# Row maxima of an attention kernel, turned by VectorE and stored by SyncE

## The chip, the cores and the metric

The kernel runs on one core of a Trainium2 chip. Five engines work side by side, each through its own list of instructions, in order: TensorE (PE, matrix products, with its weight loads shown as PEld), VectorE (DVE), ScalarE (ACT), GpSimd (POOL) and SyncE (SP, which only issues transfers). Semaphores tie them together. The metric is the device time of one execution in microseconds.

## The reference

Four layers are applied in turn, each to the layer norm of a residual stream `x` of 2048 rows and 512 columns, 32 heads of 16 columns. Layers 1 and 3 are linear attention with a learned softmax feature map; layers 2 and 4 are attention in four segments of 512 rows with a memory carried from segment to segment. The change lies in layers 2 and 4:

```
logits = jnp.einsum("bhqd,bhkd->bhqk", qs, ks) * scale + mask
p = _softmax(logits, axis=-1)
a_dot = jnp.einsum("bhqk,bhkd->bhqd", p, vs)
...
o = g * a_mem + (1.0 - g) * a_dot
```

All numbers are float32. Products that need the precision are made of a high and a low part (`hi`, `lo`; `hh`, `hl`; `oh`, `ol`), as three products.

## The kernel before, in words

**Stages.** Layer 1 (`LayerA`) makes a first pass over the rows for its sums and a second for its outputs, up to some 290 us of the profile; layer 2 (`LayerB.steps`) runs from there to some 690 us; layers 3 and 4 repeat it. The outputs of the last segment of one layer, and the first pass of the next, are done inside its neighbours.

**Slots and periods.** `LayerB.steps` counts slots `k`. Five slots make a period. A period serves one unit `m`: four heads of one segment, 32 units a layer (8 a segment). In its period, `attend` multiplies keys and queries (tile `lg`, five products, one in each slot), ScalarE takes the exponential (`P`), GpSimd clears what lies above the diagonal, and in slot 0 of the next period `weighted` multiplies by the values. Into the gaps go the projections, outputs and norms that the tables `FIRST`, `GAPS`, `LAST` and `FINAL` name: "5.2 V+/6" stands for period 5 of the segment, slot 2. The order in which the program calls an engine is the order in which it runs (`Ordered`, `held`): nothing is reordered later.

**The maxima.** The softmax needs each row's largest logit. `maxima` computes the same logits ten slots ahead of `attend`, in two pairs of PSUM banks in turn: `mx` and `my` in slots 0, 1 and 3, two of the four `g` banks in slots 2 and 4. DVE takes the maximum of each (`CUSTOM_DVE_ANT_0`, with `mxs` as the result, one column of 16 for each head and block of rows). `put_maxima` then has PE turn the 128x16 tile into 16 rows of 128 in a `g` bank; ScalarE copies them with the sign changed into `mt` (one buffer), and one slot later issues the transfer of `mt` into rows 63 and 127 of the tile `Q` of queries (shown as `e`). There the product of `attend` subtracts them, since the rows of `K` in that place hold ones. A put in slot 0 of one period is needed in slot 0 of the next.

**SyncE's list.** Six transfers a period (`stack`, slots 1 and 2, `e<-ta`) lay the parts of queries and keys in place for `attend`. Besides these it loads weights (`wqk`), rows and residuals, and stores rows. Each transfer takes the next of eight semaphores in turn and waits for the transfer that had it before.

**Paired products.** `mm3_pair` runs two products in the upper and lower 64 rows of PE. Where the two change places, at two points of 24 steps, a `sync.nop` waits for PE, and PE's next matmul waits for that `nop` (L464). So PE also waits for whatever stands ahead of it in SyncE's list.

**Residual sums.** `out_pair` multiplies by the output weights; ScalarE copies the result, GpSimd adds it to the residual two slots later, and SyncE stores the sum four slots later. The two rows of a pair are `xr` and `mmq`.

**The weights `awv`.** In layer 3's first pass, which runs inside layer 2's last segment, `load_w("awv")` issues eight loads at once ahead of the last four steps of the norm.

Of the kernel before, what the change touches and what calls it, by code (L numbers as in the profile page):

```python
# [7 lines left out]
F32 = mybir.dt.float32  # L8
F32R = mybir.dt.float32r
BF16 = mybir.dt.bfloat16  # L10
AF = mybir.ActivationFunctionType
# [4 lines left out]
D = 512  # L16
H = 32
DH = 16
P = 128
NSEG = 4  # L20
# [11 lines left out]
MT = 1  # L32
G = 4
# [68 lines left out]
def interleave_kernel(ctx, tc, x_in, a_wqkv, a_wphi, a_wo, b_wq, b_wk, b_wv, b_wo, b_beta,  # L102
                      c_ident, c_mask, c_bd, out):
    nc = tc.nc
    MUL, ADD, SUB, MAX, MIN = ALU.mult, ALU.add, ALU.subtract, ALU.max, ALU.min
# [14 lines left out]
    def T2(tag, bufs, dt=F32, shape=(P, 512)):  # L120
        return sp.tile(list(shape), dt, tag=tag, bufs=bufs, name=nm(tag))

    def PS(tag, bufs, shape=(P, 512)):
        return ps.tile(list(shape), F32, tag=tag, bufs=bufs, name=nm(tag))
# [38 lines left out]
    dve, act, pool, sync = [Ordered(e) for e in (nc.vector, nc.scalar, nc.gpsimd, nc.sync)]  # L163
# [15 lines left out]
    def tp(*a):  # L179
        work[0] += 108  # L180
        return held(nc.tensor.transpose(*a))  # L181
# [4 lines left out]
    ident = cp.tile([P, P], F32, name="ident")  # L186
    bd = cp.tile([P, 27], F32, name="bd")
# [39 lines left out]
    def load_w(key, src=None, tag="w8", low=dve):  # L227
        w = []
        for _ in bring(w, key, src, tag, low):
            pass  # L230
        return w
# [269 lines left out]
        wait(end)  # L501
        yield

    def out_pair(tiles, xdst, w, soon, w0=0, w1=D):

        pos = [PS("g", G) for _ in tiles]

        def side(po, o):
            return po[:, 0 : w1 - w0], o, lambda b, kc: w[b][:, kc, w0:w1]

        yield from mm3_pair(*[side(po, o) for po, (x, i, o) in zip(pos, tiles)])
        for po, (x, i, o) in zip(pos, tiles):
            y = T2("tb3", TB3)[:, 0 : w1 - w0]
            act.copy(y, po[:, 0 : w1 - w0])
            soon(2, lambda x=x, y=y: pool.tensor_tensor(out=x[:, w0:w1], in0=y, in1=x[:, w0:w1], op=ADD))
            if w1 == D:
                soon(4, lambda x=x, i=i: sync.dma_start(out=xdst[i], in_=x))
        yield

    def weigh(out, p, eps, add, eng=pool):  # L520
# [16 lines left out]
    def v_tile(hT, w, vv, tag, order=range(4), pairs=False):  # L537
        v = sp.tile([P, 4, VROW], F32, tag="v", bufs=2, name=nm("v"))
        vv[:] = [v]
        pool.memset(v[:, :, 0 : H * VW].rearrange("p t (h e) -> p t h e", e=VW)[:, :, :, DH : DH + 1], 1.0)  # L540
        pool.memset(v[:, :, H * VW : VROW], 0.0)
        if not pairs:
            for t in order:
                po = PS(*tag)
                yield from tok_proj(po, hT, t, w)
                act.copy(v[:, t, 0 : H * VW].rearrange("p (h e) -> p h e", e=VW)[:, :, 0:DH],
                         po.rearrange("p (h e) -> p h e", e=DH))
                yield
            return
        for ts in (order[0:2], order[2:4]):  # L550
            for n in range(pairs):
                pos = [PS(*tag) for _ in ts]
                w0, w1 = D * n // pairs, D * (n + 1) // pairs

                def side(po, t):
                    po, lhs, rhs = tok_side(po, hT, t, w)
                    return po[:, 0 : w1 - w0], lhs, lambda b, kc: rhs(b, kc)[:, w0:w1]

                yield from mm3_pair(*[side(po, t) for po, t in zip(pos, ts)])
                for po, t in zip(pos, ts):  # L560
                    act.copy(v[:, t, w0 // DH * VW : w1 // DH * VW].rearrange("p (h e) -> p h e", e=VW)[:, :, 0:DH],
                             po[:, 0 : w1 - w0].rearrange("p (h e) -> p h e", e=DH))
                yield
# [80 lines left out]
    class LayerA:  # L644
# [65 lines left out]
        def pass1(self, first):  # L710
# [8 lines left out]
            if first:  # L719
                wq, wk, wv, upc = self.first(hTs, vv, upcoming)  # L720
            else:
                norm = norm_T(self.xsrc, SEGS[0], hTs, slow=True, off=True)
                for _ in range(11):
                    next(norm)
                    yield
                wv = load_w("awv")
                for _ in norm:
                    yield
                vt = v_tile(hTs, wv, vv, ("g", G), pairs=1)

                def values():
                    for _ in range(3):
                        next(vt)

                for _ in range(5):
                    values()
                    yield
                upc = upcoming(1, False)
                next(upc[1])
                for _ in range(3):  # L740
                    values()
                    yield
                for n in range(8):
                    values()
                    yield
                wk = load_w("awk", None, "e8")
                yield
            self.mmq = [T2("mmq", 2, shape=(P, NT // 2, 2, H)) for _ in range(2)]
            kva = sp.tile([P, 8, VW], F32, tag="acc", bufs=1, name=nm("kva"))
            late = None  # L750
            for n, s in enumerate(SEGS):
# [51 lines left out]
                if n < NSEG - 1:  # L803
                    hTs, g = upc
# [176 lines left out]
    class LayerB:  # L981
# [6 lines left out]
        def start(self):  # L988
            mem = sp.tile([P, NC, 10 * VW], F32, tag="acc", bufs=1, name=nm("mem"))
            self.acc, self.kn = mem[:, :, 0 : 2 * VW], mem[:, :, 2 * VW :]  # L990
            self.sets = []
            for b in range(NSET):
                Q, K = [T2("e8", 2 * NSET, F32R, (P, 4, 512)) for _ in range(2)]
                self.sets.append((Q, K))
                for t, rows in ((Q, mask[0:32, 0:P]), (K, ones)):
                    dma(t[3:P:4].rearrange("p a t -> p (a t)"), rows.unsqueeze(1).broadcast_to([32, 16, P]))
                    yield
# [152 lines left out]
        def maxima(self, m):  # L1150


            s, c, hf = m // 8, m % 8 // 2, m % 2
            Q, K = [t[:, 2 * hf : 2 * hf + 2, :] for t in self.st[s, c]["set"]]
            mx = T2("mxs", 2, shape=(P, 16))

            def prod(pb, r, i, at, w):
                for e in range(2):
                    q, k = Q[64 * e : 64 * e + 63, r, :], K[64 * e : 64 * e + 63, r, :]
                    mm(pb[e][:, at : at + w], lhsT=q[:, i * P : (i + 1) * P], rhs=k[:, 0:w],  # L1160
                       start=True, stop=True, tile_position=(64 * e, 0))

            def top(pb, e, r, i, at):
                n = (i + 1) * P
                col = (e * 2 + r) * 4 + i
                pl = pb[e][:, at : at + n]
                with tc.high_priority():
                    dve.tensor_tensor_reduce(
                        out=pl, in0=pl, in1=mask[:, 512 - n : 512], scale=1.0, scalar=-3.0e38,
                        op0=ADD, op1=MAX, accum_out=mx[:, col : col + 1])  # L1170

            for what in ([(0, 0, 0), (0, 2, P)], [(0, 3, 0)], [(1, 0, 0), (1, 2, P)],
                         [(0, 1, 0), (1, 1, 256)], [(1, 3, 0)]):
                if self.k % R in SPARE if self.k >= 0 else self.k % 2:
                    pb = [PS("g", G) for _ in range(2)]
                else:
                    pb = [PS(t, 1) for t in ("mx", "my")]
                for r, i, at in what:
                    prod(pb, r, i, at, max(256, (i + 1) * P))
                for r, i, at in what:  # L1180
                    for e in range(2):
                        top(pb, e, r, i, at)
                self.mx[m] = mx
                yield

        def put_maxima(self, m):
            s, c, hf = m // 8, m % 8 // 2, m % 2
            Q = self.st[s, c]["set"][0][:, 2 * hf : 2 * hf + 2, :]
            pt = PS("g", G)
            tp(pt[0:16, 0:P], self.mx.pop(m), ident)  # L1190
            mt = T2("mt", MT, F32R, shape=(16, P))
            act.activation(mt, pt[0:16, 0:P], AF.Copy, scale=-1.0)
            self.later.append(lambda: act.dma_start(out=Q[63:P:64].bitcast(F32), in_=mt.bitcast(F32)))

        def attend(self, m):

# [119 lines left out]
        def out(self, s):  # L1316
            layer, i = (self.layer, NT - 4) if s < 0 else (self, 4 * s)
            for t in (0, 2):
                tiles = [(x, i + t + n, oT) for n, (oT, x) in enumerate(self.turned[0:2])]
                del self.turned[0:2]  # L1320
                parts = 2 if self.thin and s == NSEG - 2 else 1
                for n in range(parts):
                    yield from out_pair(tiles, layer.xdst, layer.wo, lambda late, f: self.at.setdefault(self.k + late, []).append(f),
                                        n * D // parts, (n + 1) * D // parts)

        def early(self):
# [269 lines left out]
```

## Time and profile before

| | us |
|---|---|
| median of three runs | 1345.33 |
| lowest and highest | 1339.39, 1346.64 |
| profiled execution | 1346.11 |
| its span, first to last instruction | 1344.4 |
| granted TensorE clock | 0.993 |
| PE, DVE, ACT, POOL busy | 1283.6, 1037.1, 845.2, 752.0 |

A group's row gives its line, engine, operation, written and read tiles and count, then busy time and the mean of one, then idle time of the engine just before and what ended it. Since a helper (L155, L177, L181) records the instructions, tiles tell more than lines. In a timeline row the first number is the start, the second the length of the merged instructions, and the bracket the idle time before them. "SPq" and "ACTq" are the issue of transfers. Matmuls overlap; their ends are modelled.

### The profile page before, as it was taken

What the parts mean: (1) busy time and instruction counts of PE and PEld (TensorE: products, weight loads), DVE (VectorE), ACT (ScalarE), POOL (GpSimd) and SP (SyncE); (2) the same over time, 40 slices, a digit from 0 to 9 for tenths busy, and PEclk for the clock granted to TensorE, in tenths of its full rate; (3) what the DMA queues carried; (4) which work ended last, traced back from release to release, by engine and by line L of the source; (5) the groups of instructions that cost most, each with busy time, mean ns of one, the idle gap of its engine ahead of it and who ended that gap; (6) DMA issues with size and microseconds to landing.
All of it is one profiled execution on the core that took longest, in us unless ns stands there. A gap on an engine that the chain in (4) does not pass through costs nothing.

```text
span 1344.4 us, 41913 instructions
## 1 busy us (share of the span) xinstructions
PE 1283.6 (95%) x16552; PEld 995.0 (74%) x16552; DVE 1037.1 (77%) x3247; ACT 845.2 (63%) x1274; POOL 752.0 (56%) x1116
## 2 busy tenths in 40 slices
PE   7999989999999999999899998999999999999987
PEld 6887868867777777776668886786767777777664
DVE  4766778688888888887667676797788788788884
ACT  5556445647787787686544433464768877877754
POOL 1568765315667667665325355561456666766643
PEclk9999999999999999999999998999999999999999
DMA  6398437535555544545350103646446554454422
GB/s 207 103 336 259 174 119 233 177 110 144 166 178 145 152 122 141 155 128 163 94 190 29 64 33 127 216 152 184 132 139 188 154 164 109 141 140 111 120 69 79
DMA packets 134419, 196.58 MB, mean 146 GB/s; under 512 B 15440, under 2 KB 61648, under 8 KB 133456
## 3 DMA queue, kind: packets, MB, share of 16 engines
q1 hardware_dynamic: 132256, 193.27, 47.6%
q8 instruction: 131, 2.15, 0.7%
q10 hardware_dynamic: 1968, 0.64, 0.2%
q14 instruction: 64, 0.52, 0.1%
HBM read 101.05 MB, written 39.85 MB: 105 GB/s over the span
## 4 chain that ended last, share of the span: by engine, by line
PE 74%; DVE 13%; ACT 4%; DMA 3%; issue 3%; POOL 2%; SPq 1%; ACTq 0%; DVEq 0%; POOLq 0%
PE g L177 58%; PE lg L177 6%; PE g L181 4%; PE mx L177 3%; DVE g L155 3%; PE lg L181 2%; DVE U L155 2%; DVE mx L155 1%; DVE my L155 1%; PE my L177 1%; ACT P L155 1%; SPq L155 1%; DVE es L155 1%; DVE mxs L155 1%; POOL P L155 1%
## 5 line engine op out<-in xcount | busy, mean ns | idle before, releaser
L155 ACT ACTIVATE P<-lg 128x1024 f32<-128x1024 f32 x316 | 321.4, 1017 | 91.6 <-PE lg L177 73.0
L155 POOL TENSOR_SCALAR_AFFINE_SELECT P<-P 128x256 f32<-128x256 f32 (+1 forms) x448 | 189.8, 442 | 265.8 <-ACT P L155 240.0
L155 DVE CUSTOM_DVE_ANT_0 mx<-mx,mask 128x512 f32<-128x512 f32 (+2 forms) x316 | 159.1, 503 | 82.6 <-PE my L177 67.5
L155 DVE CUSTOM_DVE_ANT_0 g<-g,mask 128x128 f32<-128x128 f32 (+3 forms) x392 | 189.3, 538 | 7.2 <-PE g L177 6.9
L177 PE MATMUL g<-hh,wqk 64*128 64x512 f32 (+1 forms) x960 | 183.2, 394 | 3.7 <-SPq L155 3.7
L177 PE MATMUL g<-w,oh 64*128 64x512 f32 (+2 forms) x848 | 162.0, 380 | 2.6 <-ACT oh L155 2.6
L155 DVE CUSTOM_DVE_ANT_0 my<-my,mask 128x512 f32<-128x512 f32 (+2 forms) x316 | 164.0, 519 | 0.0
L177 PE MATMUL g<-P,v 128*32 128x128 f32 (+3 forms) x2064 | 153.1, 436 | 3.0 <-DVE hl L155 1.6
L177 PE MATMUL lg<-e,e 64*128 64x512 f32 (+1 forms) x1010 | 145.6, 343 | 9.7 <-ACT P L155 9.7
L177 PE MATMUL g<-w,hh 64*128 64x512 f32 (+1 forms) x672 | 143.4, 395 | 5.3 <-SPq L155 3.3
L155 DVE DVE_READ_ACCUMULATOR2_ANT mxs<- 128x1 f32 x1024 | 144.1, 141 | 0.0
L177 PEld LDWEIGHTS lg<-e,e 64*128 64x128 f32 x1010 | 92.8, 185 | 53.5 <-ACT P L155 21.5
L177 PEld LDWEIGHTS g<-hh,wqk 64*128 64x128 f32 (+1 forms) x960 | 99.4, 185 | 24.2 <-SPq L155 6.4
L177 PEld LDWEIGHTS g<-P,v 128*32 128x32 f32 x2064 | 65.9, 110 | 65.6 <-issue 59.8
L177 PEld LDWEIGHTS g<-w,oh 64*128 64x128 f32 (+1 forms) x848 | 95.1, 187 | 19.4 <-ACT oh L155 3.5
L177 PE MATMUL g<-w,ol 64*128 64x512 f32 (+2 forms) x424 | 101.8, 377 | 0.6 <-DVE ol L155 0.5
L155 ACT COPY tb<-g 128x512 f32<-128x512 f32 (+1 forms) x132 | 71.1, 575 | 49.1 <-PE g L177 48.7
L177 PE MATMUL g<-hl,wqk 64*128 64x512 f32 (+1 forms) x480 | 101.6, 390 | 0.0
L177 PEld LDWEIGHTS g<-w,hh 64*128 64x128 f32 (+1 forms) x672 | 83.8, 188 | 21.2 <-SPq L155 3.6
L177 PE MATMUL g<-w,hl 64*128 64x512 f32 (+1 forms) x336 | 89.6, 393 | 0.9 <-issue 0.9
L155 DVE TENSOR_REDUCE es<-P 128x64 f32<-128x1024 f32 x64 | 77.4, 1209 | 13.3 <-ACT P L155 13.3
L177 PE MATMUL g<-e,e 63*128 63x256 f32 (+3 forms) x488 | 83.0, 350 | 0.9 <-DVE mxs L155 0.9
(164 smaller groups left out, 2930.3 us busy)
## 6 DMA issues: line engine op xcount, KB each, us to landing
e<-ta SPq DMA_DIRECT2D x384, 128.0 KB
wqk<-wqk SPq DMA_DIRECT2D x128, 256.0 KB
x<-x SPq DMA_DIRECT2D x48, 256.0 KB
pq<-tb SPq DMA_DIRECT2D x24, 256.0 KB
tb<-pq SPq DMA_DIRECT2D x24, 256.0 KB
x<-xr SPq DMA_DIRECT2D x22, 256.0 KB
xr<-x SPq DMA_DIRECT2D x20, 256.0 KB
x<-in SPq DMA_DIRECT2D x16, 256.0 KB
```

The lines of the kernel that those rows point to most:

```text
L155: i = f(*a, **k)
L177: return held(nc.tensor.matmul(*a, **k))
L181: return held(nc.tensor.transpose(*a))
```

## The change

**Maxima.** `maxima` now writes into one of two tiles of 128x32 that are cleared once a layer (`tops`). `put_maxima` has DVE turn four blocks of 32x32 into one 32x128 tile `mt`, in place of PE and ScalarE. SyncE issues the transfer of its first 16 rows three slots later, in place of ScalarE one slot later. The sign moves into `K`: its rows hold minus one.

**Residual sums.** `out_pair` gets the delays from outside: 2 and 5 slots (add, store) for the outputs of segments up to the second, in place of 2 and 4; 1 and 2 slots for those of the third, which run in the last segment.

**`awv`.** Its eight loads go out two at a time, behind the last four steps of the norm.

```diff
-    def out_pair(tiles, xdst, w, soon, w0=0, w1=D):
+    def out_pair(tiles, xdst, w, soon, late, w0=0, w1=D):
...
-            soon(2, lambda x=x, y=y: pool.tensor_tensor(out=x[:, w0:w1], in0=y, in1=x[:, w0:w1], op=ADD))
+            soon(late[0], lambda x=x, y=y: pool.tensor_tensor(out=x[:, w0:w1], in0=y, in1=x[:, w0:w1], op=ADD))
             if w1 == D:
-                soon(4, lambda x=x, i=i: sync.dma_start(out=xdst[i], in_=x))
+                soon(late[1], lambda x=x, i=i: sync.dma_start(out=xdst[i], in_=x))
...
-                wv = load_w("awv")
+                wv = []
+                weights = bring(wv, "awv")
                 for _ in norm:
+                    next(weights, None)
                     yield
+                for _ in weights:
+                    pass
...
+            self.tops = [T2("mxs", 2, shape=(P, 32)) for _ in range(2)]
+            for t in self.tops:
+                pool.memset(t, 0.0)
...
-            mx = T2("mxs", 2, shape=(P, 16))
+            mx = self.tops[m % 2]
...
-            pt = PS("g", G)
-            tp(pt[0:16, 0:P], self.mx.pop(m), ident)
-            mt = T2("mt", MT, F32R, shape=(16, P))
-            act.activation(mt, pt[0:16, 0:P], AF.Copy, scale=-1.0)
-            self.later.append(lambda: act.dma_start(out=Q[63:P:64].bitcast(F32), in_=mt.bitcast(F32)))
+            mt, mx = T2("mt", MT, shape=(32, P)), self.mx.pop(m)
+            for b in range(4):
+                dve.transpose(out=mt[:, 32 * b : 32 * b + 32], in_=mx[32 * b : 32 * b + 32, :])
+            self.at.setdefault(self.k + 3, []).append(
+                lambda: sync.dma_start(out=Q[63:P:64].bitcast(F32), in_=mt[0:16]))
...
+                                        (2, 5) if s < NSEG - 2 else (1, 2),
...
-    bd[[15, 31], 25] = 1.0
+    bd[[15, 31], 25] = -1.0
```

How the change moves instructions, at the places that the prediction speaks of. On PE, slot 0 of a period in layer 2 (near 410 us of the profile), before: the first products of the next unit's maxima, two groups of other turns, the turn of the maxima, the readings of the memory, the values.

```order
L177 MATMUL my_5953<-e_432_2744,e_431_2743 128x384
L181 MATMUL g_5964<-ident,x_4740 128x128 x4
L181 MATMUL g_5971<-ident,tb_922_5218 128x128 x4
L181 MATMUL g_5980<-ident,mxs_5687 16x128
L177 MATMUL g_5984<-mem_2742,tb_918_5212 32x34 x32
L177 MATMUL g_6027<-P_999_5684,v_4868 32x512 x2
```

The fourth row is gone from PE. On DVE, the same place as it stands now: the reductions of slot 0, a low part, the new turns, the weighing of the readings, and the reductions of slot 1.

```order
L155 ISA my_5955,mxs_2743<-my_5955,mask 128x384
L155 ISA mxs_2743 128x1
L155 TENSOR_TENSOR hl_5965<-g_5966,hh_5964 128x4x128
L155 STREAM_TRANSPOSE mt_5982<-mxs_2744 32x32 x4
L155 TENSOR_SCALAR r_6020<-g_5987 128x16
L155 RECIPROCAL r_6020<-r_6020 128x16
L155 TENSOR_TENSOR ot_5714<-g_5987,r_6020 128x256
L155 TENSOR_TENSOR mem_2742<-g_6049,mem_2742 128x34
L155 ISA mx_6076,mxs_2743<-mx_6076,mask 128x512
```

The turns read `mxs` of the unit before; the reductions around them write the other tile. All else stands as before. On SyncE, period 4 of layer 2's third segment (near 545 us), before:

```order
L155 DMA e_451_2825<-ta_1379_7937 32x2x512
L155 DMA x_6_104<-mmq_8226 128x512
L155 DMA x_7_105<-xr_8228 128x512
L155 DMA wqk_2393<-wqk_80 128x2x256
L155 DMA wqk_2394<-wqk_81 128x2x256
L155 DMA x_8659<-x_4_102 128x512
```

and now:

```order
L155 DMA e_453_2829<-ta_1342_7940 32x2x512
L155 DMA e_433_2747<-mt_8462 2x8x128
L155 DMA wqk_2393<-wqk_80 128x2x256
L155 DMA wqk_2394<-wqk_81 128x2x256
L155 DMA x_6_104<-mmq_8228 128x512
L155 DMA x_7_105<-xr_8230 128x512
L155 DMA x_8662<-x_4_102 128x512
```

Ahead of the two loads of weights there stands one store of maxima in place of two stores of residual sums, which went behind them.

## The prediction

> **What bounds the kernel now.** I read the page first (engines, chain), then the stages, then the tiles `mxs` and `mt` that the change takes off TensorE and ScalarE, then the waits, then single stretches of the timeline.
>
> ```profile
> span 1344.4 us, 41913 instructions
> PE 1283.6 (95%) x16552; PEld 995.0 (74%) x16552; DVE 1037.1 (77%) x3247; ACT 845.2 (63%) x1274; POOL 752.0 (56%) x1116
> PE 74%; DVE 13%; ACT 4%; DMA 3%; issue 3%; POOL 2%; SPq 1%; ACTq 0%; DVEq 0%; POOLq 0%
> ```
>
> TensorE is busy 95% of the span and carries 74% of the chain of waits. The stages say the same of the two attention layers (one call of windows; the columns are length, PE, PEld, DVE, ACT and POOL busy, granted clock, DMA share, GB/s):
>
> ```profile
> 300.00:650.00 350.00, 339.59 (x5079) 259.37 (x5076) 292.22 (x1117) 267.05 (x397) 225.74 (x368) 1.00 0.53 151
> 960.00:1250.00 290.00, 283.54 (x4249) 217.06 (x4247) 240.77 (x930) 222.99 (x330) 188.54 (x310) 1.00 0.51 143
> 1250.00:1320.00 70.00, 60.23 (x1020) 43.29 (x1018) 55.99 (x212) 43.43 (x65) 36.65 (x60) 0.98 0.35 100
> ```
>
> PE is idle 10.4 of 350 us and 6.5 of 290 us; only the last 70 us leave 9.8 us. So what shortens PE's own list shortens the kernel almost one for one, and a stall counts if PE itself stood still. DVE is the second engine: 83% of the first two stages (292.22/350, 240.77/290), with 57.8 and 49.2 us free. The whole change lies in attention, so its worth is read there.
>
> **Part 1, the transpose leaves PE.** 64 times PE turned a 128x16 tile of maxima:
>
> ```profile
> L181 PE MATMUL g<-ident,mxs x64: 272/273/278, 282.9 to 1314.0; 128*16 128x128 f32 x64
>   DVE mxs L155: 22.8, 29
> 409.68 0.60 PE L181 MATMUL g<-ident,tb 128*128 128x128 f32 x4
> 410.12 0.27 PE L181 MATMUL g<-ident,mxs 128*16 128x128 f32 x1
> 410.32 0.77 PE L177 MATMUL g<-mem,tb 128*32 128x34 f32 x64
> ```
>
> Matmuls overlap, so 273 ns is not the price; the distance of starts is. Four turns from 409.68 to 410.12 are 0.11 us each; from this one to the next matmul it is 0.20, but that step (to narrow weights) would follow the turn before it as well. I take 0.11: 64 x 0.11 = **7.0 us**; with 0.20 it would be 12.8, the upper end.
>
> The second row says what PE's matmuls and weight loads together waited for ahead of this turn: 22.8 us in 29 times for DVE's last maxima. Most of it lay beside a matmul still running. PE itself stood still this long (columns: total us, times, longest):
>
> ```profile
> PE g L181 <- DVE mxs L155: 9.1, 11, 1.6
> PE g L177 <- SPq L155: 7.0, 6, 3.3
> DVE mx L155 <- PE my L177: 67.5, 85, 3.2
> 373.65 0.28 PE L181 MATMUL g<-ident,mxs 128*16 128x128 f32 x1 [0.62 <-DVE mxs L155]
> 1277.58 0.28 PE L181 MATMUL g<-ident,mxs 128*16 128x128 f32 x1 [1.58 <-DVE mxs L155]
> ```
>
> 9.1 us in 11 waits. Without the turn PE runs on to the readings of the memory and the weighted values, some 3 us of work, before slot 1 asks for a bank that DVE must have emptied. DVE is no faster, so a part comes back there: I count **7 us** of the 9.1 as gained (0 if every wait only moves; 12 if the modelled tail of the matmul ahead, up to 0.28 us in each of the 11, was idle too).
>
> **Part 2, DVE does it.** 256 instructions of 32x32 are new. The nearest rows:
>
> ```profile
> L155 DVE STREAM_TRANSPOSE U<-U 128x512 f32<-128x512 f32 x63 | 44.5, 707 | 10.6 <-ACT U L155 10.6
> L155 DVE STREAM_TRANSPOSE U<-U 128x256 f32<-128x256 f32 x2 | 0.9, 446 | 3.8 <-ACT U L155 3.7
> 39.14 0.69 DVE L155 COPY share<-gates 32x8 f32<-32x8 f32 x4
> 525.89 0.70 DVE L155 CUSTOM_DVE_ANT_0 mx<-mx,mask 128x512 f32<-128x512 f32 x1 [1.26 <-PE my L177]
> ```
>
> From 512 to 256 columns a transpose loses 261 ns, 1.02 ns a column; 32 columns would take 446 - 224 x 1.02 = 218 ns, four of them 0.87 us. Four independent copies on 32 partitions took 0.69 us. I take 0.75 us for a put of the maxima, 48 us over 64 (44 to 56). They stand behind slot 0's reductions and ahead of slot 1's, just where DVE waits for PE: the last row shows 1.26 us of it, and the waits row 67.5 us in 85 times. So 48 us go into 107 us of idle time in two stages that also have the third. I charge **+2 us** for periods where DVE was late already (at 373.65 it was statistics of rows that delayed it); 0 is the lower bound, and the upper bound is the rival below. Where the cover is gone, it costs 0.75 us a period.
>
> The four transposes also wait for the one `mt` buffer, which is free once the store before has landed: issued in slot 3, two slots ahead. What is queued behind them on DVE is the reductions of slot 1, and for those PE waits through the banks.
>
> **Part 3, ScalarE and its store.**
>
> ```profile
> L155 ACT ACTIVATE mt<-g x64: 257/261/268, 283.3 to 1314.4; 16x128 fp32r<-16x128 f32 x64
> L155 ACTq DMA_DIRECT2D e<-mt x64: 505/520/1373, 283.6 to 1317.8; - x64
> 605.47 3.67 SPq L155 DMA_DIRECT2D w<-awv  x8
> 610.16 7.69 SPq L155 DMA_DIRECT2D e<-ta  x6
> 614.64 0.52 ACTq L155 DMA_DIRECT2D e<-mt  x1
> 615.20 1.29 ACT L155 ACTIVATE tb<-tb 128x512 f32<-128x512 f32 x2 [2.13 <-DMA w<-awv]
> 617.46 0.57 PE L177 MATMUL lg<-e,e 64*128 64x256 f32 x4 [2.06 <-ACT P L155]
> ```
>
> 64 x 0.26 = 16.7 us leave ACT, which is 76% busy in these stages and not the bound: no gain of its own. But the stretch from 605 shows a stall. Eight loads of `awv` go out in 3.67 us; ScalarE's store of the maxima then waits for a transfer of that burst (2.13 us idle), the exponentials behind it are late, and PE stands 2.06 us. The change takes both away: the store is no longer on ScalarE, and the loads go out as two, two and four in three periods. **2 us** gained (0 to 2.1). What they feed is asked for only some slots later.
>
> **Part 4, SyncE's queue.** It takes the 64 stores, 0.52 us each on ScalarE's queue (its neighbours' issue has a median of 0.59, the row of `e<-ta` below). That would be idle business, were it not for L464: the halves of a paired product are separated by an empty instruction on SyncE, and PE waits for it when the queue is behind. These are the 7.0 us in 6 waits above. Three of them:
>
> ```profile
> 542.00 0.53 SPq L155 DMA_DIRECT2D x<-mmq  x1
> 542.78 1.41 SPq L155 DMA_DIRECT2D x<-xr  x1
> 544.28 0.94 SPq L155 DMA_DIRECT2D wqk<-wqk  x2
> 545.33 0.50 PE L177 MATMUL g<-hh,wqk 64*128 64x512 f32 x2 [0.97 <-SPq L155]
> 1000.02 0.53 SPq L155 DMA_DIRECT2D x<-mmq  x1
> 1000.82 2.10 SPq L155 DMA_DIRECT2D x<-xr  x1
> 1004.06 0.50 PE L177 MATMUL g<-hh,wqk 64*128 64x512 f32 x2 [1.68 <-SPq L155]
> 642.45 0.53 SPq L155 DMA_DIRECT2D x<-mmq  x1
> 643.61 4.37 SPq L155 DMA_DIRECT2D x<-x  x4
> 648.08 0.50 PE L177 MATMUL g<-w,hh 64*128 64x512 f32 x2 [3.28 <-SPq L155]
> L155 SPq DMA_DIRECT2D e<-ta x384: 526/589/1698, 255.3 to 1296.5; - x192
> ```
>
> At 545 and 1004 the stores of two residual sums (0.53 + 1.41 and 0.53 + 2.10 us) stand ahead of the weights' loads and the empty instruction. A slot later they stand behind it, and one store of maxima (0.5) takes their place: 1.0 + 1.6 us gained. At 648 four loads of rows take 4.37 us, and two of them read rows whose stores went out 1 to 2 us earlier (642.45); in the last segment the change issues these stores two slots earlier, ahead of six stack transfers, so I count 2 of the 3.28 us. Against it: the other three waits (1.1 us together) and those empty instructions that had less than 0.55 us to spare get the new 0.5 us; I charge 2 us. Net **2.5 us** gained (from 5 lost to 6 gained).
>
> **Sum:** 7.0 + 7 - 2 + 2 + 2.5 = 16.5 us. The profiled execution took 1346.11 us, 1.7 over its span and 0.8 over the median of the runs shown: 1346.1 - 16.5 = 1329.6, and 1328.8 beside the median. I say **1328**.
>
> **Rivals.** First, the waits only move: DVE has 48 us more to do and PE's 9.1 us come back at the banks of slots 1 and 3, with SyncE's gains eaten by its new stores. What is left is 7.0 + 2 - 2 = 7: 1339. For it: DVE at 83% goes to 90%. Against: the 67.5 us in which DVE waits for PE. The Trainium skill (Perfetto Trace Analysis, Optimizing Scalar/DVE Operations) holds that many small instructions cost a saturated VectorE throughput, which speaks for this one; no row here shows DVE saturated in the long stages.
>
> Second, slower: SyncE's queue becomes the bound. If the store of slot 3 delays the second empty instruction of every period, PE waits 0.55 us in some 60 of the 64 periods: 33 us lost, against 14 gained in parts 1 to 3 and 4.6 at the three places. That is 14.4 slower than 1345.3, about 1360. It decides from the point where SyncE comes less than 0.55 us ahead of PE. Against: only 6 waits now, and 384 x 0.59 + 128 x 0.47 = 287 us of issue in some 745 us of attention leave SyncE waiting most of the time. The Trainium skill (Perfetto Trace Analysis, DMA Optimizations) advises to spread transfers over the issuing engines where an issuer is the bottleneck, the opposite of this step; its condition is not met by these rows.
>
> Third, all of it comes: every one of the 9.1 us, 0.2 us a turn (12.8), 2, 6 and no charge on DVE: 30 us, 1316.
>
> That the change doesn't do it is excluded: no transpose of `mxs` and no store on ScalarE stands in the new order.
>
> **Chances.** Forecast (1320 to 1337) 0.55, third (below 1320) 0.19, first (1337 to 1344) 0.16, second 0.10. The range takes in the third's end and the first: 1314 to 1343. A measurement of this kernel tells about 0.5%, 6.7 us, from no change, so faster means below 1338.6: 0.55 + 0.19 and a quarter of the first's, 0.78; same, the rest of the first's, 0.12; slower 0.10.
>
> **What would show it.** Right: four DVE transposes of about 0.2 us each in every period, no `mxs` among what PE waits for at L181, PE's waits for SyncE below 4 us, the periods near 545, 612 and 1004 shorter by 1 to 2 us, and an ordinary period shorter by 0.1. Wrong: new waits of PE for `mxs` at `mx`, `my` or `g` of 5 us and more (the first rival), waits for SyncE above 10 us (the second), or the first product of a period (`lg<-e,e`) waiting for the transfer of `mt`, which I priced at nothing because it has two slots to land.

## The result, and the profile after

The changed kernel takes 1330.23 us (median of 4 runs, 1329.09 to 1334.12), beside 1345.99 us for the kernel before (1339.39 to 1348.97). The ratio is 0.9895, 95% interval 0.9853 to 0.9937: faster, by about 16 us. The profiled execution, the slowest of the four, took 1334.12 us with a span of 1332.4 us, 12.0 us under the span before. The number came out close to the forecast, but not by the forecast's sum, as the trace shows.

The page of the changed kernel: span, busy time by engine, chain by engine. Then its three stages of the attention layers (length, PE, PEld, DVE, ACT and POOL busy, granted clock, DMA share, GB/s):

```profile
span 1332.4 us, 41983 instructions
...
PE 1276.0 (96%) x16488; PEld 989.9 (74%) x16488; DVE 1077.4 (81%) x3503; ACT 834.8 (63%) x1210; POOL 752.4 (56%) x1120
...
PE 75%; DVE 16%; ACT 3%; issue 3%; DMA 2%; POOL 1%; SPq 1%; DVEq 0%; ACTq 0%; POOLq 0%
```

```profile
300.00:650.00 350.00, 346.49 (x5228) 264.32 (x5226) 318.58 (x1269) 269.16 (x378) 228.51 (x375) 1.00 0.54 154
960.00:1250.00 290.00, 288.61 (x4412) 221.44 (x4406) 263.41 (x1054) 227.03 (x320) 195.89 (x319) 1.00 0.53 149
1250.00:1320.00 70.00, 62.98 (x1004) 45.69 (x1002) 57.51 (x216) 45.53 (x62) 39.24 (x68) 1.00 0.32 87
```

In the first two stages PE is idle 3.5 of 350 us and 1.4 of 290 us, where it was 10.4 and 6.5. DVE rose from 83% to 91%. PE has 64 instructions fewer, ScalarE 64 fewer, DVE 256 more. Here are the new instructions, from the view of the tile `mt` (ns at least, median, at most), and what PE itself stood still for (total us, times, longest):

```profile
L155 DVE STREAM_TRANSPOSE mt<-mxs x256: 189/199/207, 285.3 to 1303.6; 32x32 f32<-32x32 f32 x128
L155 SPq DMA_DIRECT2D e<-mt x64: 508/549/638, 286.2 to 1308.8; - x64
```

```profile
PE mx L177 <- DMA e<-ta: 8.3, 2, 4.2
PE lg L177 <- ACT P L155: 7.5, 19, 1.3
...
PE g L177 <- DVE mxs L155: 3.8, 10, 0.9
PE lg L177 <- DMA e<-mt: 2.9, 3, 1.3
...
PE g L181 <- DVE mxs L155: 1.5, 6, 0.3
...
PE g L177 <- SPq L155: 0.7, 3, 0.3
```

Two waits of the kernel before are gone: 9.1 us for `mxs` at the turn, and all but 0.7 of the 7.0 us for SyncE. Waits for `mxs` at products that use the banks came up, 3.8 and 1.5 us. And there are two waits for transfers that the kernel before does not have at all: 8.3 us in only two times for a stack transfer, and 2.9 us in three for the store of the maxima.

To see where the time went, I measured both traces by the distance between successive ScalarE copies of the weighted values (`U<-g`), one for each period of attention:

| stretch | after against before |
|---|---|
| up to the first period of the first attention layer | +7.7 us |
| its periods | -11.6 us |
| up to the first period of the second attention layer | +6.5 us |
| its periods and the end | -14.7 us |

So some 26 us were gained inside the attention layers, and 14 were lost just ahead of them.

**The loss.** SyncE's own queue at the start of the first attention layer, in the kernel before, and below it in the changed one. The last row is from the list of what SyncE waits for in the changed kernel (total us, times, longest):

```profile
278.45 0.33 SPq L155 DMA_DIRECT2D x<-xr  x1
278.87 6.56 SPq L155 DMA_DIRECT2D e<-ta  x9
```

```profile
279.37 0.33 SPq L155 DMA_DIRECT2D x<-xr  x1
286.16 0.64 SPq L155 DMA_DIRECT2D e<-mt  x1
286.86 5.69 SPq L155 DMA_DIRECT2D e<-ta  x9
...
SPq L155 <- DVE mt L155: 12.8, 2, 6.4
```

VectorE and PE of the changed kernel in the same microseconds:

```profile
282.53 0.46 DVE L155 CUSTOM_DVE_ANT_0 g<-g,mask 128x256 f32<-128x256 f32 x1
...
284.96 0.42 DVE L155 TENSOR_TENSOR ot<-g,r 128x256 f32<-128x256 f32 x1
285.30 0.83 DVE L155 STREAM_TRANSPOSE mt<-mxs 32x32 f32<-32x32 f32 x4
...
288.09 0.50 PE L177 MATMUL lg<-e,e 64*128 64x512 f32 x2 [1.25 <-DMA e<-mt]
292.65 0.55 PE L177 MATMUL mx<-e,e 63*128 63x256 f32 x1 [4.05 <-DMA e<-ta]
```

The first store of the maxima is in SyncE's list ahead of nine stack transfers. Its data is ready only when VectorE has done the four transposes, at 286.1; before that VectorE has the reductions of the second unit (from 282.53) and divisions of the other layer's rows. So SyncE stands still from 279.7 to 286.2 (one of the two waits for `mt` in the last row above), and nine transfers, which left from 278.87 before, leave from 286.86. PE waits 1.25 us for the maxima and then 4.05 us for the stacks. The second attention layer starts with the same two waits, 1.2 and 4.2 us. In this lead-in, before the first period, slots are short: the reductions from 282.53 belong to slot -9, where the put stands, and the product at 288.09 to slot 0, so that nine slots pass in under 6 us, where a period of five takes 12. "Three slots on" is 7 us in the steady state and some 2 us here.

### The profile page after: what moved, and what is told of

The parts are those of the page before. It is cut to its first block, busy times and chain, and to the rows that moved or that the text cites. A ratio compares the mean times of both kernels' runs of the same rounds, so it can differ in the third digit from the quotient of the medians.

```text
span 1332.4 us, 41983 instructions
## 1 busy us (share of the span) xinstructions
PE 1276.0 (96%) x16488; PEld 989.9 (74%) x16488; DVE 1077.4 (81%) x3503; ACT 834.8 (63%) x1210; POOL 752.4 (56%) x1120
## 4 chain that ended last, share of the span: by engine, by line
PE 75%; DVE 16%; ACT 3%; issue 3%; DMA 2%; POOL 1%; SPq 1%; DVEq 0%; ACTq 0%; POOLq 0%
PE g L177 59%; PE lg L177 6%; PE g L181 4%; PE mx L177 3%; DVE g L155 3%; DVE U L155 2%; DVE mx L155 2%; DVE my L155 2%; PE lg L181 2%; PE my L177 1%; DVE es L155 1%; ACT P L155 1%; DVE mxs L155 1%; SPq L155 1%; DMA P<-in 1%
## 5 line engine op out<-in xcount | busy, mean ns | idle before, releaser
L177 PE MATMUL mx<-e,e 63*128 63x256 f32 (+3 forms) x323 | 83.1, 320 | 8.4 <-DMA e<-ta 8.3
```

What stands on the lines that cost most here:

```text
L177: return held(nc.tensor.matmul(*a, **k))
```

## The experiments

Every one of these was timed beside the kernel before, whose median was 1343.3 to 1344.2 us in those runs. I call the changed kernel "the change".

**1. The first transposes early.** The put of the first unit moves from slot -9 to slot -12. SyncE's list stays as in the change: only four transposes in each attention layer stand elsewhere in VectorE's list.

```
-          ... -11: "v2", -9: "max0"}
+          ... -12: "max0", -11: "v2"}
```

> Only the four transposes of the first unit of each attention layer move: on VectorE they now stand right behind that unit's own last maxima, three slots earlier, ahead of the second unit's reductions and of the first divisions of the other layer's rows. SyncE's list is as in the changed kernel. Theory (the store stands ahead of nine stack transfers in SyncE's list and holds them until VectorE has turned the maxima): the starts of the two attention layers lose what they lost, 7.7 + 6.5 = 14.2 us, but for a us or so, PE's waits for e<-ta at mx fall from 8.3 us to below 1, those for e<-mt at lg from 2.9 to below 1, and the time is 1316 to 1320. Rival (the stack transfers were late by themselves, or VectorE's extra work there is what PE waits for): the waits stay or turn into waits for mxs, and the time stays at 1327 to 1332.

Measured: 1315.92 us, ratio 0.979 (0.9766 to 0.9813), span 1314.2. That is 14 us faster than the change by the medians, 18.2 by the spans of the two profiled executions. Both starts are 9.7 and 7.3 us shorter than in the change. SyncE's queue and two stretches of this kernel at the start:

```profile
277.96 0.64 SPq L155 DMA_DIRECT2D e<-mt  x1
278.66 14.19 SPq L155 DMA_DIRECT2D e<-ta  x12
```

The row of twelve holds the same nine, which go out up to 284.4, and three that follow from 291.0. The granted clock is the third figure from the end:

```profile
286.00:288.00 2.00, 2.00 (x10) 1.65 (x9) 1.93 (x10) 0.31 (x1) 0.41 (x1) 1.00 0.00 0
288.00:290.00 2.00, 2.00 (x14) 1.41 (x15) 1.93 (x9) 1.30 (x2) 0.00 (x0) 1.00 0.00 0
```

PE is busy throughout, the wait for `e<-ta` does not show any more, and the one for `e<-mt` fell from 2.9 to 0.3 us. The store is in the same place of the same list; with its data ready it holds nobody. The theory held, at its lower end. Of the versions that give the kernel's output this is the fastest, and it beats both kernels.

**2. The first store on ScalarE's queue.** VectorE's list is that of the change.

```
-  lambda: sync.dma_start(out=Q[63:P:64]...
+  lambda q=act if m == 0 else sync: q.dma_start(out=Q[63:P:64]...
```

> VectorE's order is that of the changed kernel; only the first unit's store in each attention layer goes out from ScalarE's queue instead of SyncE's. Theory (place in SyncE's list): the stack transfers leave on time, the 8.3 us at mx go, the wait for e<-mt at lg (2.9 us) stays since the transposes are as late as before; 1319 to 1323. Rival (it is the lateness of the transposes on VectorE by itself, whatever queue the store is on): above 1327.

Measured: 1323.8 us, ratio 0.9845 (0.9824 to 0.9867), span 1318.4.

```profile
280.44 0.33 SPq L155 DMA_DIRECT2D x<-xr  x1
280.87 6.06 SPq L155 DMA_DIRECT2D e<-ta  x9
```

```profile
PE lg L177 <- DMA e<-mt: 2.5, 2, 1.3
```

The stack transfers leave at once and the 8.3 us are gone, although the transposes are as late as in the change; only the wait for the maxima themselves is left. Both starts are as short as in the kernel before (+0.1 and -1.1 us by the same measure as in the table). The median, 6.4 us below the change, lies 0.8 us above the range of the theory and below the rival's 1327. With the first experiment this settles it: what cost the time was a store with late data at the head of SyncE's list, and what stood behind it.

**3 and 4. The two parts alone.** One has only the maxima's part (residual sums and last weights' load as before), the other only the rest (PE turns, ScalarE copies and stores the maxima).

```
 3:  -soon(late[0], ...) ... soon(late[1], ...)      +soon(2, ...) ... soon(4, ...)
     -weights = bring(wv, "awv") ... next(weights, None)      +wv = load_w("awv")
 4:  -dve.transpose(out=mt[:, 32 * b : 32 * b + 32], ...)     +tp(pt[0:16, 0:P], self.mx.pop(m), ident)
     -self.at...append(lambda: sync.dma_start(out=Q[63:P:64]...   +self.later.append(lambda: act.dma_start(out=Q[63:P:64]...
```

> The part on the maxima alone: the residual sums and the last weights' load are as in the kernel before. The starts of the layers lose their 14 us as in the changed kernel. Theory (the prediction's parts are separate): the places at 545, 648 and 1004 keep their waits for SyncE, 1.0 + 2.9 + 1.7 = 5.6 us by the periods of the two traces, so 1335 to 1337; the stall near 612 goes or becomes a wait for e<-mt. Rival (the moved stores of the residual sums are worth nothing by themselves, the maxima's turn brings it all): 1328 to 1332.

> The other part alone: residual sums later, the last weights' load spread; the maxima are turned by PE and stored by ScalarE as in the kernel before. The layer starts lose nothing. Theory: 5.6 us from the residual sums and 2.4 from the stall near 617 are gained, 1336 to 1339. Rival (these gains come only where SyncE's list also has the maxima's store, or move to the next wait): 1342 to 1347, no difference from the kernel before.

Measured: 1335.54 us (0.9937, 0.9917 to 0.9956) for the maxima alone, 1336.12 us (0.9939, 0.992 to 0.9957) for the rest alone. Against the 1343.31 us of the kernel before in those runs they gain 7.8 and 7.2 us; the sum, 15.0, is about what the whole change gains (15.8), and each gain is uncertain by 2 to 3 us. Both times lie in the ranges of the theories. In the second one the periods at 545, 617, 648 and 1004 us of the kernel before are shorter by 0.8, 2.2, 2.1 and 1.2 us, and PE waits 1.6 us for SyncE where it waited 7.0. The first gains so little because it carries the whole loss of the starts:

```profile
PE mx L177 <- DMA e<-ta: 8.2, 2, 4.1
...
PE g L177 <- SPq L155: 4.7, 8, 1.4
```

Place by place the parts do not add up, and here the theory for the first one had a premise wrong. It let the waits for SyncE at 545, 648 and 1004 stay; but with the residual sums as before they fall from 0.97, 3.28 and 1.68 us to 0.46, 1.36 and 0.50, and in the second one to nothing, 1.17 and 0.44. Either part alone takes most of them; why the first one does was not followed up. Of the other five of its eight waits, 0.4 to 0.5 us each, four lie in periods in which PE did not wait for SyncE before.

**5. PE or VectorE.** As experiment 1, but PE turns and ScalarE copies, with the store on SyncE in the change's slot.

```
...
-  for b in range(4):
-      dve.transpose(out=mt[:, 32 * b : 32 * b + 32], in_=mx[32 * b : 32 * b + 32, :])
+  pt = PS("g", G)
+  tp(pt[0:16, 0:P], self.mx.pop(m), ident)
...
+  act.activation(mt, pt[0:16, 0:P], AF.Copy, scale=-1.0)
...
```

> As e1_early, but the maxima are turned by PE through the identity and copied by ScalarE, as before the change; the store stays on SyncE three slots on, and the first put of a layer is three slots early. Beside e1_early this prices the move from PE to VectorE alone. Theory (the prediction's parts 1 and 2: 7.0 for the turns, 7 for waits, less 2 for VectorE): 12 us slower, 1325 to 1331, PE's waits for mxs at the turn 7 to 10 us. Rival (the gain came from the store leaving ScalarE and from the other edits): 1316 to 1320.

Measured: 1336.67 us, ratio 0.9947 (0.9928 to 0.9966), span 1334.2: 20.8 us slower than experiment 1 by the medians, 20.0 by the spans. The expectation said 12. The rows of K hold plus one again, and the turn takes a bank `g` again. The turn's place in the waits of PE:

```profile
PE g L181 <- DVE mxs L155: 11.0, 14, 1.6
```

By the pages PE is busy for 1277.3 us here and for 1268.4 in experiment 1, so 8.9 of the 20.0 us are busy time and 11.1 idle time. The 8.9 make 0.14 us for each of the 64 turns, inside the 0.11 to 0.20 that the rows before the change allowed. Period by period, 22 are longer by 0.1 to 0.2 us, 14 by 0.3 to 0.5 and 13 by 0.7 to 1.3. On balance PE gains about as much idle time as the waits at the turn hold: experiment 1 has 5.0 us of waits for `mxs` at the banks in their place, but other small waits of PE are missing there. The rival, no difference from experiment 1, is out.

**6 and 7. VectorE's share, up and down.** Both start from experiment 1. One does each transpose twice, the other leaves two of four out (its `mt` is one tile, made and cleared at the start of a layer).

```
 6:  +for _ in range(2):
          dve.transpose(out=mt[:, 32 * b : 32 * b + 32], ...)
 7:  -for b in range(4):
     +for b in range(2):
 ...
```

> As e1_early, with each of the four transposes done twice: 256 more of 0.2 us on VectorE, 0.85 us a period, 54 us in all; the results are the same. Prices a transpose of VectorE that the prediction charged at 2 us for the first 48. Theory (they lie in the time in which VectorE waits for PE, 36 us for mx yet): up to 4 us slower, 1316 to 1320. Rival (VectorE, now 91 per cent busy in the long stages, sets the pace of many periods): 8 to 40 us slower, 1324 or more.

> As e1_early, with two of the four transposes of each put left out (half of the rows go without their maxima, so the output is another): 128 instructions of 0.2 us fewer on VectorE, 27 us. With e6_dve_twice (54 us more cost 25.6) it tells whether VectorE's time is hidden up to the changed kernel's amount. Theory (the reserve ends close above it: the turn from PE gave 20.8 us, nothing of it paid back): 0 to 3 us faster, 1313 to 1316. Rival (every microsecond on VectorE costs about half of itself, here too): 10 to 15 us faster, 1301 to 1306.

Measured: twice, 1341.49 us (0.9975, 0.996 to 0.999), 25.6 us slower than experiment 1; half, 1315.29 us (0.9791, 0.9774 to 0.9807), the same as experiment 1 within the intervals, as its theory had it. The first long stage in the one with half of them, and in the one with twice as many (the fourth figure is DVE's busy time):

```profile
300.00:650.00 350.00, 346.73 (x5266) 265.04 (x5255) 307.78 (x1212) 269.37 (x377) 228.70 (x376) 1.00 0.54 152
```

```profile
300.00:650.00 350.00, 344.60 (x5131) 267.06 (x5133) 334.03 (x1349) 264.73 (x372) 225.43 (x368) 1.00 0.54 151
```

From 88% (half) to 91% (experiment 1 has 319.85 of 350) no cost of VectorE's time shows. From there to 95% the next 54 us cost 25.6: two thirds of the periods are longer, most by 0.1 to 0.9 us and seven by 1.2. The theory for "twice" (up to 4 us) fell, its rival held. Where between 91 and 95% the cost begins was not tried; the change lies below that point. The wait that tells how near it is, is VectorE's own for PE (`mx<-PE my`): 67.5 us before, 38.8 with half, 26.4 in experiment 1 and 4.9 with twice. These are the rows of the half one and of experiment 1:

```profile
DVE mx L155 <- PE my L177: 38.8, 63, 1.6
```

```profile
DVE mx L155 <- PE my L177: 26.4, 62, 0.9
```

**8 and 9. SyncE's share.** Both from experiment 1 again, with a second store behind each one: first to the same rows, then to a place of its own.

```
 8:  lambda: [sync.dma_start(out=Q[63:P:64]..., in_=mt[0:16]) for _ in range(2)]
 9:  lambda: [sync.dma_start(out=Q[63:P:64]..., in_=mt[0:16]),
              sync.dma_start(out=dtile((16, P), nm("spare")), in_=mt[0:16])]
```

> As e1_early, with each store of the maxima issued twice: 64 more issues of 0.55 us in SyncE's list, in the slot that the second rival of the prediction speaks of. Theory (SyncE stands well ahead of PE at most of the empty instructions): up to 4 us slower, 1316 to 1320, PE's waits for SyncE at most 5 us. The prediction's second rival (0.5 us a period at the empty instructions): 20 to 33 us slower, 1336 and more.

> As e1_early, with a second store of the same maxima behind each one, to a place in DRAM that nobody reads or writes else: 64 more issues in SyncE's list, without the wait for the store before that e7_store_twice had (its second store wrote the same rows and so waited 84 us for the first). The honest price of the issue. Theory (some 30 of 126 empty instructions follow less than 0.55 us of idle time on SyncE): up to 6 us slower, 1316 to 1322. The prediction's second rival (0.55 us in every period): 33 us slower, about 1349.

Measured: 1379.37 us (1.0253, 1.023 to 1.0276) to the same rows, 63.5 us slower than experiment 1; 1322.26 us (0.9843, 0.9826 to 0.9859) to its own place, 6.3 us slower (4.3 by the spans). The first was to price 0.55 us of issue and did something else. These are its waits on SyncE's queue and on PE:

```profile
SPq L155 <- DMA e<-mt: 84.0, 64, 2.4
```

```profile
PE g L177 <- SPq L155: 49.4, 51, 2.1
```

The second store of the same rows waits until the first has landed, 1.3 us each time, and holds the empty instructions behind it. The other one shows the price of one more issue on SyncE here, 0.07 to 0.1 us of the kernel's time for 0.55 us of the queue, just above the range of its theory and far from the rival's 33 us. Of the 4.3 us by the spans, 1.5 are a single wait of PE for a load of weights (`mx` for `w<-bwo`), which is not in experiment 1. PE's wait for SyncE is 2.2 us, beside 0.8 in experiment 1:

```profile
PE g L177 <- SPq L155: 2.2, 7, 0.7
```

**10. The store one slot after the transposes.**

```
-  self.at.setdefault(self.k + 3, []).append(lambda: sync.dma_start(out=Q[63:P:64]...
+  self.at.setdefault(self.k + 1, []).append(lambda: sync.dma_start(out=Q[63:P:64]...
```

> As e1_early, but every store of the maxima stands in SyncE's list one slot after the transposes instead of three. Prices the slots in between. Theory (a store whose data is not ready holds all that stands behind it in SyncE's list, as at the layer starts): SyncE waits for VectorE in most periods, the empty instructions of slots 1 and 2 and the stack transfers come late, 5 to 20 us slower than e1_early (1321 to 1336), with PE waiting for SyncE 5 us or more. Rival (only the layer starts are so tight; by slot 1 the transposes are done): 1314 to 1319.

Measured: 1327.09 us, ratio 0.9877 (0.9862 to 0.9892), 11.2 us slower than experiment 1.

```profile
PE g L177 <- SPq L155: 9.2, 17, 1.0
```

The theory held. Of the 12.1 us by the spans, 2.0 and 2.5 us lie ahead of the first periods of the two layers, the rest mostly in single periods that are 0.3 to 1.0 us longer. PE's wait for SyncE is 0.8 us in 3 times with three slots (experiment 1). So the distance of three slots keeps most of this kind of wait out of the steady state.

**11. All stores on ScalarE's queue**, three slots on, from experiment 1.

```
-  lambda: sync.dma_start(out=Q[63:P:64]...
+  lambda: act.dma_start(out=Q[63:P:64]...
```

> As e1_early (the first transposes early), but all 64 stores of the maxima go out from ScalarE's queue, in the same slots (three after the transposes). Beside e1_early (1315.9) this prices the queue alone. Theory (ScalarE has 25 per cent idle, in slot 3 the data is long ready, so nothing blocks there): within 4 us of e1_early, 1312 to 1320. Rival (each store holds ScalarE for its issue of 0.5 us ahead of exponentials for which PE waits, 7.6 us in 19 waits for P already): slower by 5 us or more, above 1321.

Measured: 1318.23 us, ratio 0.9803 (0.9778 to 0.9828). The theory, within 4 us of experiment 1, held. The interval overlaps that of experiment 1, so which of the two queues has the store decides nothing that can be told here. What matters is whether the data is there when its turn comes.

## Why the prediction was right, and where it was wrong

The time (1328 forecast, 1330.23 measured) and the sign were right. The sum was not: two errors of about equal size and opposite sign met. Parts 1, 2 and 4 bring some 11 us more than the prediction counted, and a loss of 14 us that it did not have stands against them. That 1330 came out beside 1328 was luck; the 1328 itself is the sum's 1328.8, rounded down.

**The step that failed** is the one on the wait that the change adds. The prediction looked for what is queued behind the waiting instruction in the steady state only: for VectorE it named the reductions of slot 1, for SyncE the empty instructions, and it priced the landing of `mt` at nothing "because it has two slots to land". It did not follow the first put, in slot -9, where slots take some 0.6 us and nine stack transfers stand behind the store. That cost 14 us in the change. Experiment 1 gives them back; experiment 2 gives back 6.4 by the medians, and both starts by its profile. The sign that it named as "wrong", `lg<-e,e` waiting for the transfer of `mt`, did appear (2.9 us in 3 times), but the larger wait, 8.3 us, was for what stood behind that transfer. The second rival came near, with a store in SyncE's list that holds others. But it had the store hold them by its issue of 0.55 us, at the empty instruction of every period; what the runs show is a store that waits for its data, at two places.

**Part 1** was sized too small. It counted 7.0 us for the turns and 7 of the 9.1 us of waits. Experiment 5 measures 20 us for the turn's move, VectorE's new work included. The reason for holding back 2 us was that PE would meet the same lateness at the banks. It does, with new waits for `mxs` of 3.8 + 1.5 us in the change, but other waits of PE shrink by as much, so on balance nothing is held back.

**The signs.** Two of the prediction's signs misled here. The new waits for `mxs` at `g` come to 5.3 us, over the 5 that were to speak for the first rival, though experiment 5 rules that rival out. And `mxs` is still among what PE waits for at L181 (1.5 us), at turns of other tiles.

**Part 2**: 0.83 us for four transposes against 0.75, 53 us against 48 (44 to 56). That they lie beside other work is right for the second half of them: half cost the same as all (experiments 1 and 7). Whether the 2 us charged were paid is below what these runs can tell. The upper bound, VectorE as the limit, is real but starts further on (experiment 6).

**Part 3**: 2 us for the stall near 617; the period is shorter by 2.35 us in the change. The size was right. The prediction named two edits for it; either one alone is enough. The period is 2.2 us shorter in experiment 4, which spreads the loads and leaves the store on ScalarE, and as short as in the change in experiment 3, which does the opposite.

**Part 4**: the gains at 545, 1004 and 648 were put at 1.0, 1.6 and 2 us; in the change these periods are shorter by 1.0, 1.7 and 2.9. The 2 us charged for the new stores do not show in the change's waits for SyncE (0.7 us in all). They do in experiment 3, whose four new waits sum to 1.8 us; there the residual sums are as before. With all the stores on ScalarE's queue (experiment 11) the kernel is no faster. So the net was 5 to 6 us rather than 2.5, near its upper end. But the moved residual sums are not the only reason: the same waits fall by more than half in experiment 3, which the prediction did not foresee.

The third rival, "all of it comes" (1316, with a chance of 0.19), comes close for the attention layers: without the loss at the starts nearly the same kernel takes 1315.92 (experiment 1). The first rival, that waits only move, is out.

## What to carry to other kernels

When a store, or any instruction that waits for another engine, goes into an in-order list, write down what stands behind it at every place where the list is used, and above all in the fill of the pipeline, where "three slots later" can be a third of what it is in the steady state. An engine at 91% can still take work for nothing and at 95% charge half of it, so the measure is the time for which it waits for the critical engine, not its share. And a price is measured with an operation that shares nothing with the first one: a second store to the same rows measured the wait for the first.

## What the runs showed of the hardware that was not expected

**A stall of PE can cost more than itself, by the clock.** After the wait that ends at 292.65 the change's PE runs at half its clock for about 6 us (columns as in the stages above; the clock is the third figure from the end):

```profile
290.00:292.00 2.00, 0.00 (x0) 0.00 (x0) 0.01 (x1) 0.00 (x0) 0.14 (x1) 0.98 0.87 202
292.00:294.00 2.00, 1.35 (x5) 1.03 (x6) 0.44 (x3) 0.00 (x0) 0.00 (x0) 0.50 0.84 193
...
296.00:298.00 2.00, 2.00 (x6) 1.52 (x6) 0.00 (x0) 0.00 (x0) 0.00 (x0) 0.50 0.04 8
298.00:300.00 2.00, 2.00 (x13) 1.20 (x13) 0.36 (x1) 1.03 (x2) 0.00 (x0) 0.81 0.00 0
300.00:302.00 2.00, 2.00 (x24) 1.75 (x22) 1.32 (x7) 1.16 (x2) 0.41 (x1) 1.00 0.00 0
```

Three of the same products take 1.28 us there (294.93 to 296.21) and 0.69 us in experiment 1 (286.43 to 287.12). The change, then experiment 1:

```profile
294.93 1.05 PE L177 MATMUL g<-w,hh 128*128 128x512 f32 x2
...
296.21 1.05 PE L177 MATMUL g<-w,hh 128*128 128x512 f32 x2
```

```profile
286.43 0.62 PE L177 MATMUL g<-w,hh 128*128 128x512 f32 x2
...
287.12 0.62 PE L177 MATMUL g<-w,hh 128*128 128x512 f32 x2
```

From the windows and those after the second stall (0.50 and 0.68 from 944 to 948) I estimate that the clock took 4 to 5 us of the 14 lost. The Trainium skill (TensorE: Matmul & The Clock Gate, Why this matters for your kernels) says to leave no gap of PE above some 3 us, or the clock falls to half; the gaps of 4.05 and 4.2 us agree. But a shorter one did it too: in the kernel before, PE stood still 1.58 us at 1277.58, and the clock fell; in experiment 4 the same wait (at 1270.58) left it alone. In experiment 4 this period is 1.6 us shorter than in the kernel before. The rows of the kernel before, then of experiment 4:

```profile
1278.00:1280.00 2.00, 2.00 (x72) 0.97 (x61) 1.76 (x8) 1.06 (x2) 0.41 (x1) 0.54 0.04 8
1280.00:1282.00 2.00, 2.00 (x28) 1.11 (x20) 0.00 (x0) 0.00 (x0) 0.00 (x0) 0.60 0.00 0
```

```profile
1270.00:1272.00 2.00, 1.42 (x73) 1.01 (x77) 2.00 (x11) 1.11 (x2) 1.81 (x3) 1.00 0.06 13
1272.00:1274.00 2.00, 2.00 (x33) 0.99 (x24) 0.75 (x4) 0.25 (x2) 0.41 (x1) 1.00 0.03 8
```

And the longest of PE's waits for SyncE in the kernel before, 3.28 us up to 648.08, was followed by a clock of 1.00. So in these traces the length of the gap alone does not decide.

The record of the clock in the thirteen traces (two kernels, eleven experiments) says more. In each trace the granted clock changes only at points that lie multiples of 3.41 us apart. Between 100 and 1300 us it goes from full to half 31 times, and in the 3.41 us before such a point PE was busy for 0 to 54% of the time. Of some 4500 such stretches that kept the full clock, only nine had less than 54%, the lowest 45%. So it counts how a stall lies on this grid. The 1.58 us of the kernel before fell into one stretch (1274.76 to 1278.17, PE busy for 1.60 us). The same wait in experiment 4 lay across two, with 2.46 and 2.31 us busy. The 3.28 us also lay across two, with 1.51 and 2.04. The first of these is a little emptier than the stretch that lost the clock, so the busy share of the profile is not the whole rule. No run was made to test it.
